# Relative-bias attention followed by hash-routed experts: rows stored in order and gathered through an id table, bias rows written from 128 partitions

## The chip, the cores and the metric

The kernel runs on one core of a Trainium2 chip. The metric is the device time of one execution in microseconds (us). Before the change it is 440.38 us, the median of three runs (440.21 to 440.39).

A core has five engines that run side by side, each with its own queue of instructions, and that wait for each other through semaphores: TensorE (PE, matrix products into PSUM), VectorE (DVE), ScalarE (ACT), GpSimd (POOL) and SyncE (SP, here only for issuing DMAs). DMAs are issued from the queues of SP, ACT and POOL and are carried out by 16 DMA engines. A DMA with a list of row numbers (an indirect DMA, a gather or a scatter) is issued from POOL.

## What is computed

```python
# q, k, v: [8, 8, 576, 64] float32; bias_table: [32, 8]; token_ids: [4608] int64
# w1: [8, 512, 1024], w2: [8, 1024, 512] float32
scores = scale * np.matmul(q, k.transpose(0, 1, 3, 2))
...
scores = scores + bias.transpose(2, 0, 1)[None, :, :, :]   # by |i - j|, constant from 128 on
attn = np.exp(scores - np.max(scores, axis=-1, keepdims=True))
attn = attn / (np.sum(attn, axis=-1, keepdims=True) + 1e-09)
attn_out = np.matmul(attn, v)
x = np.ascontiguousarray(attn_out.transpose(0, 2, 1, 3)).reshape(B * S, H * D)
expert_idx = token_ids * np.int64(2654435761) % np.int64(E)
for e in range(E):
    mask = expert_idx == e
    h = np.maximum(x[mask] @ w1[e], 0.0)
    out[mask] = h @ w2[e]
```

So 4608 tokens of width 512 come out of attention, and each goes through one of eight experts, chosen by a hash of its id. With eight experts and an odd multiplier, the expert's weights can be permuted or the low three bits of the id taken; the kernel takes the low three bits.

## The kernel before

**Attention half.** The work is cut into 32 pairs of heads (`pairs`, batch by batch, four per batch). For pair n the loop body calls `scores(n, g)` five times: TensorE computes a block of scores into PSUM, and ScalarE takes the exponential into `att` (four times, L406) or `atts` (once, L418). VectorE then multiplies the band near the diagonal by the exponential of the bias (`band`, L439 and L445). Beyond the band the bias is constant and cancels. `av_steps(n - 1)` runs the products with v of the pair before (L472), interleaved into the same body, and VectorE normalises into `x_all` (L482, L483). Further per pair: `load(n + 4)` issues seven DMAs for q, k and v on SP; `cast_k` and `cast_q` on VectorE and `cast_v` on ScalarE turn them to float16 two and three pairs ahead; `transpose_q` and `transpose_k` bring them into place through PSUM slots named `aux`, of which there are two. `load_vs` and `cast_vs` (SP and POOL, L218) bring the last 64 rows of v for the next batch.

**Order.** The attention half is emitted under a manual schedule for all five engines: each engine runs its instructions in the order in which the program writes them. An instruction that waits holds up what follows in its own queue, and nothing else. An engine whose instructions wait for nothing runs ahead of the loop body in which they are written.

**The bias.** The table is expanded to 8 rows (one per head), its exponential taken (`ebsb`, L580), and each row written 64 times, with a shift that grows by one element, into the DRAM tensor `t5_f` (L586, two DMAs of 512 KB, from 8 partitions, on ACT's queue). Reading `t5_f` back with another stride gives the diagonal bands `ebd` and `ebs` (L602 and L607, eight DMAs on SP). They stand on SP ahead of `load(2)` and `load(3)`, and `cast_k(2)`, `cast_q(2)` and `cast_q(3)` stand on VectorE ahead of most of pair 0's bands.

**Routing.** `route_load` (pair 4) fetches the low words of the ids, 4 bytes at a time, into `te` with tokens on partitions. `route` (a generator, one step for each `scores` call in pairs 6 to 11) computes the expert of each token and its rank within the expert, and from these the slot `ds2` of each of the 40 groups of 128 tokens. An expert has 640 slots.

**Rows to experts.** `x_all` rows carry two extra float16 columns that hold the token's number. Ten DMAs (`fill_table`, L629, pairs 2 to 11, on SP) fill the table `t5_xperm` in DRAM with zero rows and an impossible number. `dispatch` (L498, 40 indirect DMAs on POOL, two per pair from pair 12) scatters x rows of finished batches to their slots; the last five follow the last pair. In the expert half `x_load` (L724, on SP) reads the 640 slots of an expert as one block, `x_transpose` turns it (L738, L742), TensorE computes both layers (L759, L777), and each block of 128 result rows is scattered to `out` (L785, 40 indirect DMAs on POOL) with the numbers that came along in the row. Weights are loaded and cast by POOL's DMAs (L132, L138); experts 0 and 1 during attention (pairs 20, 22, 25, 28), later ones two experts ahead.

A last part, under `tc.If(over > 0)`, serves tokens beyond 640 of an expert. With these inputs it doesn't run.

Of the kernel before, what the change touches and what calls it, by code (L numbers as in the profile page):

```python
# [31 lines left out]
def kernel(  # L32
# [28 lines left out]
    NROW = NSLOT + N  # L61
# [5 lines left out]
    XW = DM + 2  # L67
# [28 lines left out]
    TOK_np = TOK_np.reshape(P, NGT)  # L96
# [8 lines left out]
    TOK_d = nc.inline_tensor(TOK_np, "t5_tok")  # L105
# [3 lines left out]
    F_d = nc.dram_tensor("t5_f", [H * P + 1, PW], F16, kind="Internal")  # L109
    xperm_d = nc.dram_tensor("t5_xperm", [NROW, XW], F16, kind="Internal")  # L110

# [4 lines left out]
    tok = cst.tile([P, NGT], I32, name="tok")  # L116
# [37 lines left out]
    with tc.tile_pool(name="at", bufs=1) as at, tc.tile_pool(  # L154
# [7 lines left out]
        x_all = at.tile([P, B, NIT, XW], F16, name="x_all")  # L162
# [7 lines left out]
        te = at.tile([P, NGT], I32, name="te")  # L170
# [76 lines left out]
        def route_load():  # L247
            tid32 = moe_token_ids.bitcast(I32)
            for t in range(NIT):
                tk = tok_of[i_first[t] : i_first[t] + P]  # L250
                p0 = 0
                while p0 < P:
                    p1 = p0 + 1
                    while p1 < P and tk[p1] == tk[p1 - 1] + 2:
                        p1 += 1
                    nc.sync.dma_start(
                        out=te[p0:p1, B * t : B * t + B].unsqueeze(2),
                        in_=bass.AP(tid32.tensor, 2 * int(tk[p0]),
                                    [[4, p1 - p0], [2 * S, B], [1, 1]]),
                    )  # L260
                    p0 = p1

        def route():
            nc.gpsimd.tensor_copy(
                out=x_all[:, :, :, DM:XW].bitcast(I32),
                in_=tok[:, :].rearrange("p (t b) -> p b t", b=B).unsqueeze(3),
            )
            nc.vector.tensor_scalar(
                out=te[:, :], in0=te[:, :], scalar1=E - 1, scalar2=None,
                op0=ALU.bitwise_and,  # L270
            )
            yield
            nc.vector.tensor_tensor(
                out=ef[:, :], in0=te[:, :], in1=msk[:, :NGT], op=ALU.add
# [61 lines left out]
            dlt = at.tile([P, NGT], F32, name="dlt")  # L336
            nc.vector.scalar_tensor_tensor(
                out=dlt[:, :], in0=tok[:, :], scalar=float(NSLOT),
                in1=sel[:, :], op0=ALU.add, op1=ALU.subtract,
            )  # L340
            yield
            nc.vector.tensor_tensor(
                out=dlt[:, :], in0=dlt[:, :], in1=ovf[:, :], op=ALU.mult
            )
            yield
            nc.vector.tensor_tensor(
                out=ds2[:, :], in0=dlt[:, :], in1=sel[:, :], op=ALU.add
# [149 lines left out]
        def dispatch(b, t):  # L497
            sc_in = nc.gpsimd.indirect_dma_start(  # L498
                out=xperm_d.ap()[:, :],
                out_offset=bass.IndirectOffsetOnAxis(  # L500
                    ap=ds2[:, B * t + b : B * t + b + 1], axis=0
                ),
                in_=x_all[:, b, t, :],
                in_offset=None,
                bounds_check=NROW - 1,
                oob_is_err=False,
            )
            disjoint(sc_in, "xrows")
# [13 lines left out]
        for hh in range(2):  # L522
            nc.scalar.dma_start(
                out=tbl[:, :, hh : hh + 1],
                in_=bias_table[:, NPAIR * hh : NPAIR * hh + NPAIR].unsqueeze(2),
            )
        ohsb = at.tile([NB, FW], F32, name="ohsb")
        nc.scalar.dma_start(out=ohsb[:, :], in_=OH_d.ap())
        nc.scalar.dma_start(out=ident[:, :], in_=I128_d.ap())

# [42 lines left out]
        for i in range(2):  # L573
            nc.tensor.matmul(
                out=bps[:H, i, :FH],
                lhsT=tbl[:, :, :].rearrange("n m h -> n (m h)"),
                rhs=ohsb[:, FH * i : FH * i + FH],
            )
        ebsb = at.tile([H, 2, FH], F16, name="ebsb")
        nc.scalar.activation(  # L580
            out=ebsb[:, :, :], in_=bps[:H, :2, :FH], func=AF.Exp, bias=0.0,
# [3 lines left out]
        for r in range(2):  # L585
# [3 lines left out]
                    [[P * PW, H], [2 * PW + 1, D], [1, 2 * FY]],  # L589
                ),  # L590
                in_=ebf[:, (1 - r) * FY : (3 - r) * FY]
                .unsqueeze(1).to_broadcast([H, D, 2 * FY]),
            )
        transpose_q(0)
# [4 lines left out]
        for hh in range(2):  # L599
            for o in range(2):  # L600
                f0 = hh * P * PW + o * FY + MAXD // 2 - 1
                nc.sync.dma_start(  # L602
                    out=ebd[:, :, hh, o, :],
                    in_=bass.AP(F_d.ap().tensor, f0,
                                [[PW, P], [2 * P * PW, NPAIR], [1, WB]]),
                )
                nc.sync.dma_start(  # L607
                    out=ebs[D * hh : D * hh + D, :, o, :],
                    in_=bass.AP(F_d.ap().tensor, f0,
                                [[PW, D], [2 * P * PW, NPAIR], [1, UB]]),  # L610
                )
        load(2)
        load(3)
        cast_vs(0)
# [5 lines left out]
        nc.sync.dma_start(out=tok[:, :], in_=TOK_d.ap())  # L620
        zx = at.tile([P, 4, XW], F16, name="zx")
        nc.gpsimd.memset(zx[:, :, :DM], 0.0)
        nc.gpsimd.memset(zx[:, :, DM:XW].bitcast(I32), BIG)

        FILLS = 10

        def fill_table(i):
            rows = NSLOT // FILLS
            nc.sync.dma_start(  # L629
                out=xperm_d.ap()[rows * i : rows * (i + 1), :].rearrange(  # L630
                    "(p r) d -> p (r d)", p=P
                ),
                in_=zx[:, :, :].rearrange("p r d -> p (r d)"),
            )

        NP = len(pairs)
        waiting = []
        routing = route()

        def finish(its):  # L640
            for t in its:
                dispatch(B - 1, t)

        for n in range(NP + 1):
# [8 lines left out]
            if n == 4:  # L653
                route_load()
            if 2 <= n < 2 + FILLS:
                fill_table(n - 2)
# [7 lines left out]
            if n >= 5 and pairs[n - 1][1] == 0:  # L664
                waiting += [(pairs[n - 5][0], t) for t in range(NIT)]
            if n >= 12:
                for _ in range(2):
                    if waiting:
                        dispatch(*waiting.pop(0))
# [8 lines left out]
            for g in range(NIT):  # L678
                scores(n, g)
                if 6 <= n < 12:  # L680
                    next(routing, None)
                if g == 0:
                    if 0 < n < NP - 1:
# [16 lines left out]
                elif g == 3:  # L700
                    if n == 0:
                        transpose_q(1)
                        transpose_k(1)
# [8 lines left out]
        assert not waiting  # L712
        guard.__exit__(None, None, None)

    with tc.tile_pool(name="mo", bufs=1) as mo, tc.tile_pool(
# [6 lines left out]
        def x_load(e):  # L722
            xpn = mo.tile([P, NSC, XW], F16, name="xpn", bufs=3)
            nc.sync.dma_start(  # L724
                out=xpn[:, :, :],
                in_=xperm_d.ap()[ts(e, CAP), :].rearrange(
                    "(sc p) d -> p sc d", p=P
                ),
            )
# [15 lines left out]
        with tc.manual_schedule(engines={mybir.EngineType.SP}):  # L745
            xn = {0: x_load(0)}
# [182 lines left out]
```

## Time and profile before

| what | value |
|---|---|
| median of three runs | 440.38 us |
| the profiled execution, its own time | 437.86 us |
| its span, first to last instruction | 436.0 us |
| TensorE busy | 334.5 us (77%) |
| VectorE busy | 225.9 us (52%) |
| ScalarE busy | 219.7 us (50%) |
| POOL busy | 106.8 us (24%) |
| attention half | up to about 263 us |
| expert half, from the first transpose of a block (L738) | from 275.53 us |

The rows that follow are the page's second part: the span in 40 slices of 10.9 us, one digit for each. A digit is the busy share of the slice in tenths, 9 being 90% or more. `DMA` is the mean busy share of the 16 DMA engines, and `GB/s` what they moved.

```profile
PE   4120788789865585898888780799999999999991
ACT  1110699889954495898889680133150422404220
POOL 2020010000056125041322204014335053350421
DMA  7438789899999468779799102548999999998211
```

The rows show four parts: a start of some four slices in which hardly anything is busy but the DMA engines; an attention part with dips in slices 12 to 16 and 23; a bridge of about two slices (25 and 26); and an expert part in which TensorE is always busy. A busy share is no limit by itself: in the attention part VectorE and ScalarE are both near full where the pace is steady, and the pace of a pair is read from ScalarE's exponentials.

### The profile page before, as it was taken

The numbers are of one execution on the slowest core, as the hardware profiler recorded it, in microseconds if no ns is written. First come the engines' busy times: TensorE is split into PE (matmuls) and PEld (weight loads), VectorE is DVE, ScalarE is ACT, GpSimd is POOL, SyncE is SP. The second block draws the span as 40 slices with busy tenths as digits, with TensorE's granted clock in tenths as the row PEclk, the third lists the DMA queues.
The fourth block names the chain that finished last, engine by engine and source line by source line (L and its number), as shares of the span: only waits on it lengthen the run. The fifth ranks groups of instructions, "written<-read, shape, count | busy, mean of one in ns | idle before, by whom it ended". The sixth has DMA issues, their size and how long they took to land. (4 is left out here: it accounts for less than half of the span.)

```text
span 436.0 us, 8653 instructions
## 1 busy us (share of the span) xinstructions
PE 334.5 (77%) x3398; PEld 238.0 (55%) x3398; DVE 225.9 (52%) x608; ACT 219.7 (50%) x258; POOL 106.8 (24%) x135
## 2 busy tenths in 40 slices
PE   4120788789865585898888780799999999999991
PEld 1010677667744474776667570566575665656550
DVE  4001699999953594898989561121413223142221
ACT  1110699889954495898889680133150422404220
POOL 2020010000056125041322204014335053350421
PEclk9999999999996697999999897699999999999997
DMA  7438789899999468779799102548999999998211
GB/s 171 61 44 205 186 212 161 215 251 248 247 226 252 106 163 183 179 158 215 185 208 172 43 2 65 172 68 196 162 241 244 164 256 156 251 213 164 108 50 71
DMA packets 130803, 72.75 MB, mean 167 GB/s; under 512 B 88992, under 2 KB 121888, under 8 KB 130753
## 3 DMA queue, kind: packets, MB, share of 16 engines
q1 hardware_dynamic: 111568, 39.97, 39.4%
q0 software_dynamic: 17664, 30.96, 33.3%
q10 hardware_dynamic: 1520, 1.18, 2.1%
q8 instruction: 28, 0.46, 0.4%
q14 instruction: 23, 0.18, 0.1%
HBM read 68.38 MB, written 22.06 MB: 207 GB/s over the span
## 5 line engine op out<-in xcount | busy, mean ns | idle before, releaser
L406 ACT ACTIVATE att<-ps 128x1152 f16<-128x1152 f32 x128 | 140.7, 1128 | 44.4 <-remote 15.5
L398 PE MATMUL ps<-qt,kz 128*128 128x384 f16 x256 | 78.1, 344 | 34.7 <-ACT att L406 30.7
L765 ACT ACTIVATE h<-hps 128x640 f16<-128x640 f32 x64 | 45.1, 704 | 113.2 <-PE hps L759 112.5
L472 PE MATMUL px<-vt,att 128*128 128x98 f16 x1280 | 84.6, 211 | 2.8 <-issue 1.4
L472 PEld LDWEIGHTS <-att 128*128 128x128 f16 x1280 | 72.4, 101 | 9.0 <-issue 2.8
L759 PE MATMUL hps<-xpt,w1t 128*128 128x320 f16 x512 | 72.8, 303 | 0.0
L777 PE MATMUL ops<-w2t,h 128*128 128x512 f16 x320 | 72.7, 379 | 0.0
L439 DVE TENSOR_TENSOR att<-att,ebd 128x512 f16<-128x512 f16 (+1 forms) x192 | 68.4, 385 | 0.7 <-ACT att L406 0.5
L402 PE MATMUL ps<-qt,kz 128*128 128x192 f16 x256 | 65.7, 257 | 0.0
L759 PEld LDWEIGHTS <-w1t 128*128 128x128 f16 x512 | 50.7, 99 | 21.6 <-issue 0.2
L498 POOL DMA_INDIRECT t_xperm<-x_all,ds x40 | 40.0, 1001 | 82.1 <-DVE x_all L483 40.4
L742 DVE COPY xpt<-xps 128x640 f16<-128x640 f16 x32 | 15.0, 489 | 74.6 <-PE xps L738 73.6
L785 POOL DMA_INDIRECT out_dram<-ok,xpn x40 | 39.2, 980 | 57.4 <-DVE ok L784 50.9
L784 DVE COPY ok<-ops 128x512 f32<-128x512 f32 x40 | 27.7, 692 | 47.0 <-PE ops L777 47.0
L777 PEld LDWEIGHTS <-h 128*128 128x128 f16 x320 | 30.7, 98 | 33.5
L402 PEld LDWEIGHTS <-kz 128*128 128x128 f16 x256 | 25.9, 101 | 40.4 <-issue 39.9
L218 POOL CAST vs<-vsf 64x256 f16<-64x256 f32 x16 | 7.7, 484 | 128.2 <-DMA vsf<-in_v_dram 100.8
L358 PE MATMUL pq<-ident,qh 96*128 96x96 f16 x192 | 14.5, 215 | 29.0 <-DVE qt L366 20.3
L472 PE MATMUL px<-vs,atts 128*128 128x132 f16 x160 | 36.1, 225 | 0.5 <-ACT atts L418 0.3
L240 ACT ACTIVATE vt<-vf 128x512 f16<-128x512 f32 x32 | 19.8, 623 | 31.1 <-DMA vf<-in_v_dram 31.1
L234 DVE CAST kh<-kf 128x640 f16<-128x640 f32 x32 | 15.6, 487 | 34.7 <-DMA kf<-in_k_dram 34.6
L398 PEld LDWEIGHTS <-kz 128*128 128x128 f16 x256 | 26.1, 102 | 13.2 <-issue 2.7
(56 smaller groups left out, 272.9 us busy)
## 6 DMA issues: line engine op xcount, KB each, us to landing
qf<-in_q_dram SPq DMA_DIRECT2D x64, 144.0 KB
kf<-in_k_dram SPq DMA_DIRECT2D x64, 128.0 KB
vf<-in_v_dram SPq DMA_DIRECT2D x64, 128.0 KB
w1t<-in_moe_w_dram POOLq DMA_DIRECT2D x8, 1024.0 KB
w2t<-in_moe_w_dram POOLq DMA_DIRECT2D x8, 1024.0 KB
t_xperm<-zx SPq DMA_DIRECT2D x10, 514.0 KB
xpn<-t_xperm SPq DMA_DIRECT2D x8, 642.5 KB
kf<-in_k_dram SPq DMA_DIRECT2D x32, 32.0 KB
```

The source lines that it names most:

```text
L240: nc.scalar.activation(out=vt[n % 4][:, :].rearrange("p (h y) -> p h y", h=2)[:, :, : NDUO * VN].rearrange("p h (t x) -> p h t x", t=NDUO) ...
L398: nc.tensor.matmul(out=ps[:, hh, :QW], lhsT=kt, rhs=qt[:, :QW], start=True, stop=True,)
L402: nc.tensor.matmul(out=ps[:, 2, RW * hh : RW * hh + RW], lhsT=kt, rhs=qt[:, QW:], start=True, stop=True,)
L406: nc.scalar.activation(out=att[:, g, :, :], in_=ps[:, :, :QW], func=AF.Exp, bias=0.0, scale=scale,)
L439: nc.vector.tensor_tensor(out=a, in0=a, in1=ebd[:, m, :, :, a0 + w0 : a1 + w0], op=ALU.mult,)
L472: nc.tensor.matmul(out=px[:, ii, o : o + w], lhsT=lhsT, rhs=rhs, start=(y == 0), stop=(y == len(todo) - 1), skip_group_check=True,)
L498: sc_in = nc.gpsimd.indirect_dma_start(out=xperm_d.ap()[:, :], out_offset=bass.IndirectOffsetOnAxis(ap=ds2[:, B * t + b : B * t + b + 1], ...
L759: nc.tensor.matmul(out=hps[:, nr, :NR], lhsT=w1h[:, kt, ts(ft, P)], rhs=xt[e][:, kt, ts(nr, NR)], start=(kt == 0), stop=(kt == NPT - 1),)
L765: nc.scalar.activation(out=h1[:, ft, :].rearrange("p (r n) -> p r n", r=NRC), in_=hps[:, :, :NR], func=AF.Relu, bias=0.0, scale=1.0,)
L777: nc.tensor.matmul(out=ops[:, :], lhsT=h1[:, ft, ts(kc, P)], rhs=w2h[:, ft, :], start=(ft == 0), stop=(ft == NFT - 1),)
L784: nc.vector.tensor_copy(out=ok[:, :], in_=ops[:, :])
L785: so = nc.gpsimd.indirect_dma_start(out=out[:, :], out_offset=bass.IndirectOffsetOnAxis(ap=xn[e][:, kc, DM:XW].bitcast(I32), axis=0), in_= ...
```

## The change

- **Bias.** The table is repeated to 128 columns (`tblr`: eight heads, 16 copies), so the exponential comes out on 128 partitions. Each partition writes 4 shifted rows to `t5_f`. The bytes are the same. The reading back is split: `load_bias(0, 1)` for the first head pair of each batch, then `load(2)`, then `load_bias(1, NPAIR)`, then `load(3)`, eight DMAs for each `load_bias`. `cast_vs(0)` and, in pair 0, `transpose_q(1)` and `transpose_k(1)` move forward.
- **Ids.** One DMA on ACT's queue loads all ids as 8 rows (`raw`). VectorE masks them, converts them to float16, and TensorE transposes them (`tps`). `route` runs from pair 2 to 7, and its last three steps become one.
- **Rows.** `x_all` loses its two extra columns. Finished batches are stored in token order into `t5_x` by SP (`store`, two DMAs a batch, three for the last). A small table `t5_id` of 5120 slots with two numbers each is filled with an impossible number in one DMA. `name_slot` scatters the pair (row number, token number) of each of the 40 groups into it: 40 indirect DMAs on POOL, three per pair from pair 8. In pair 24 SP loads the table back as `xid`.
- **Expert half.** `x_load` becomes five indirect gathers on POOL per expert, from `t5_x` into one of three tiles `xg`, which are zeroed at the start. The result scatter takes its numbers from `xid`. The manual schedule for SP around the first two loads goes.

```diff
-    F_d = nc.dram_tensor("t5_f", [H * P + 1, PW], F16, kind="Internal")
-    xperm_d = nc.dram_tensor("t5_xperm", [NROW, XW], F16, kind="Internal")
+    NRP = P // H
+    RPW = P // (2 * NRP)
+    PP = RPW * (2 * PW + 1)
+    HPF = NRP * PP
+    F_d = nc.dram_tensor("t5_f", [P + 1, PP], F16, kind="Internal")
+    x_d = nc.dram_tensor("t5_x", [N, DM], F16, kind="Internal")
+    id_d = nc.dram_tensor("t5_id", [NSLOT, 2], I32, kind="Internal")
...
-        def route_load():
...
+        def route():
+            for h0, w, u0 in ((0, UA, 0), (QW, UB, UA)):
+                nc.vector.tensor_scalar(
+                    out=te[:, h0 : h0 + 2 * w].rearrange(
+                        "b (o u) -> b o u", o=2
+                    ),
+                    in0=raw[:, :, 0].rearrange("b (u o) -> b o u", o=2)[
+                        :, :, u0 : u0 + w
+                    ],
+                    scalar1=E - 1, scalar2=None, op0=ALU.bitwise_and,
+                )
+            yield
+            nc.gpsimd.memset(tef[:, :].bitcast(I32), 0)
+            nc.vector.tensor_copy(out=tef[:B, :], in_=te[:, :])
+            yield
+            tps = aux([P, NIT, P], F16, "tps")
             for t in range(NIT):
...
+                nc.tensor.transpose(
+                    out=tps[:, t, :], in_=tef[:, i_first[t] : i_first[t] + P],
+                    identity=ident[:, :],
+                )
...
-        def dispatch(b, t):
-            sc_in = nc.gpsimd.indirect_dma_start(
-                out=xperm_d.ap()[:, :],
+        def name_slot(g):
+            i = nc.gpsimd.indirect_dma_start(
+                out=id_d.ap()[:, :],
                 out_offset=bass.IndirectOffsetOnAxis(
-                    ap=ds2[:, B * t + b : B * t + b + 1], axis=0
+                    ap=ds2[:, g : g + 1], axis=0
                 ),
-                in_=x_all[:, b, t, :],
+                in_=pay[:, g, :],
                 in_offset=None,
-                bounds_check=NROW - 1,
+                bounds_check=NSLOT - 1,
                 oob_is_err=False,
             )
...
+        def store(b, t0, t1):
+            xv = x_d.ap()[S * b : S * b + S, :]
+            t2 = min(t1, NDUO)
+            nc.sync.dma_start(
+                out=xv[P * t0 : P * t2, :].rearrange("(t p) d -> p t d", p=P),
+                in_=x_all[:, b, t0:t2, :],
+            )
+            if t1 > NDUO:
+                nc.sync.dma_start(
+                    out=xv[NB4:, :], in_=x_all[P - S + NB4 :, b, NDUO, :]
+                )
...
-                    [[P * PW, H], [2 * PW + 1, D], [1, 2 * FY]],
+                    [[PP, P], [2 * PW + 1, RPW], [1, 2 * FY]],
                 ),
                 in_=ebf[:, (1 - r) * FY : (3 - r) * FY]
-                .unsqueeze(1).to_broadcast([H, D, 2 * FY]),
+                .unsqueeze(1).to_broadcast([P, RPW, 2 * FY]),
...
+        cast_vs(0)
+        load_bias(0, 1)
         load(2)
+        load_bias(1, NPAIR)
         load(3)
-        cast_vs(0)
...
+        nobody = at.tile([P, NSLOT // P, 2], I32, name="nobody")
+        nc.gpsimd.memset(nobody[:, :, :], BIG)
+        nc.sync.dma_start(
+            out=id_d.ap().rearrange("(p g) c -> p (g c)", p=P),
+            in_=nobody[:, :, :].rearrange("p g c -> p (g c)"),
+        )
+        for i in range(3):
+            nc.gpsimd.memset(xg[i][:, :, :].bitcast(I32), 0)
...
         def finish(its):
-            for t in its:
-                dispatch(B - 1, t)
+            store(B - 1, its[0], its[-1] + 1)
...
-            if n == 4:
-                route_load()
-            if 2 <= n < 2 + FILLS:
-                fill_table(n - 2)
...
             if n >= 5 and pairs[n - 1][1] == 0:
-                waiting += [(pairs[n - 5][0], t) for t in range(NIT)]
-            if n >= 12:
-                for _ in range(2):
-                    if waiting:
-                        dispatch(*waiting.pop(0))
+                store(pairs[n - 5][0], 0, NIT)
+            if n >= 8:
+                for g in unnamed[:3]:
+                    name_slot(g)
+                del unnamed[:3]
+            if n == 24:
+                nc.sync.dma_start(
+                    out=xid[:, :, :],
+                    in_=id_d.ap().rearrange("(g p) c -> p g c", p=P),
+                )
...
         def x_load(e):
-            xpn = mo.tile([P, NSC, XW], F16, name="xpn", bufs=3)
-            nc.sync.dma_start(
-                out=xpn[:, :, :],
-                in_=xperm_d.ap()[ts(e, CAP), :].rearrange(
-                    "(sc p) d -> p sc d", p=P
-                ),
-            )
+            xpn = xg[e % 3]
+            for sc in range(NSC):
+                nc.gpsimd.indirect_dma_start(
+                    out=xpn[:, sc, :],
+                    out_offset=None,
+                    in_=x_d.ap()[:, :],
+                    in_offset=bass.IndirectOffsetOnAxis(
+                        ap=xid[:, NSC * e + sc, 0:1], axis=0
+                    ),
+                    bounds_check=N - 1,
+                    oob_is_err=False,
+                )
             return xpn
```

## The prediction

> **What bounds the kernel now.** I read the slices and the chain of waits first, then stretches of equal pace, then the order of time in the two places where the pace breaks.
>
> ```profile
> 262.56 0.32 POOL t_xperm L498
> ...
> 267.67 2.42 DMA t_xperm<-x_all,ds
> ...
> 270.52 4.36 DMA xpn<-t_xperm
> 274.88 0.66 issue
> 275.53 0.70 PE xps L738 x5
> ```
>
> The chain reaches back only to 260 us. From 275.53 on it is TensorE without gaps (the expert half, 152 us). Between the halves lies a bridge: five scatters, a landing, a load, 13 us. What precedes must be read by pace. Each head pair issues four `att` exponentials (L406), one `atts` and one `vt`: 4 x 1.13 + 0.65 + 0.62 = 5.8 us of ScalarE.
>
> ```profile
> core 0: us, ACT busy (x), PEclk, DMA share, GB/s
> 55.80:79.10 23.30, 17.61 (x16) 1.00 0.90 186
> 79.10:105.10 26.00, 17.61 (x16) 1.00 1.01 241
> 105.10:122.50 17.40, 13.21 (x12) 1.00 0.97 243
> 122.50:149.30 26.80, 8.93 (x8) 0.78 0.98 217
> 149.30:162.00 12.70, 8.80 (x8) 0.92 0.49 119
> 162.00:180.10 18.10, 8.92 (x8) 0.81 0.88 191
> 180.10:234.40 54.30, 39.44 (x36) 1.00 0.90 187
> 234.40:255.50 21.10, 13.21 (x12) 0.92 0.30 63
> ```
>
> These are L406 alone by stretch; four are one pair. First row: 4 pairs in 23.3 us, 5.8 each, so there ScalarE is the limit, with the DMA engines 0.90 busy. The last five rows hold 72 = 18 pairs, worth 104.4 us, in 133.0: 28.6 us too many. In that stretch lie 35 of the 40 row scatters (L498).
>
> ```profile
> 137.77 0.62 ACT L240 ACTIVATE vt<-vf 128x512 f16<-128x512 f32 x1
> 145.99 2.15 ACT L406 ACTIVATE att<-ps 128x1152 f16<-128x1152 f32 x2 [7.59 <-remote]
> ```
>
> ScalarE stands for 7.59 us while POOL issues eight scatters back to back (134.40 to 144.41, one per 1.28 us); TensorE's last matmul for that tile began at 138.13. The runs differ: 14 scatters in runs of six and eight lie where 15.2 us are lost, six (and a weight load) where 6.5 are lost, so 1.08 each; ten in runs of one to three cost 0.2 each; five in one run 3.7 us, 0.74 each. The mean is 28.6/35 = 0.8. What stands still is TensorE's word to the others.
>
> The Trainium skill ("SBUF — State Buffer", Who interferes with whom) says that TensorE and ScalarE wait on nobody, and that DMAs never contend with compute engines. The 7.59 us disagree. By that rule small scatters would be free and the sum 401, which is a rival below.
>
> ```profile
> 8.71 11.88 ACTq L586 DMA_DIRECT2D t_f<-ebsb  x2
> 20.68 1.15 ACT L240 ACTIVATE vt<-vf 128x512 f16<-128x512 f32 x2 [12.01 <-DMA vf<-in_v_dram]
> ...
> 42.95 0.63 ACT L240 ACTIVATE vt<-vf 128x512 f16<-128x512 f32 x1 [19.07 <-DMA vf<-in_v_dram]
> ...
> 51.12 1.13 ACT L406 ACTIVATE att<-ps 128x1152 f16<-128x1152 f32 x1 [1.51 <-PE ps L402]
> ```
>
> ```profile
> 31.79 0.38 SPq L602 DMA_DIRECT2D ebd<-t_f  x1
> ...
> 36.64 0.60 SPq L185 DMA_DIRECT2D qf<-in_q_dram  x1
> ```
>
> The third place is the start. The bias rows (2 x 512 KB from 8 partitions) are issued at 8.71, and SP gets past its wait for them at 31.79: 23.1 us, 45 GB/s. ACT's queue is held, and on SP everything behind the wait is late: load(2), for which VectorE waits until 41.72, and load(3), until 44.80. Steady work begins with the exponential at 51.12.
>
> **The change, part by part.** The sum is made against the profiled execution, 437.86 us with 436.0 of span. The median of the runs is 440.38; I add the difference, 2.5.
>
> *Bias rows from 128 partitions.* Same bytes. At the best slice's 252 GB/s they take 4.2 us, at the expert load's pace (642.5 KB in 4.36 us, 151 GB/s) 7.0; the upper end is the 23.1 of now, if the partitions were not the limit. I take 5.8, landing at X = 14.5 us, since other full-width transfers here run at such rates. Behind X, SP issues eight bias loads for pair 0 (31.79 to 36.64 now: 4.85), load(2) (4.06), eight more bias loads (4.85), and load(3), whose second q part is issued 1.56 later and lands 2.54 after that (42.26 to 44.80 now). `cast_q(3)` stands ahead of band(0,1) on VectorE, so pair 0 goes on at X + 17.9, where it now goes on at 31.79 + 13.0. From there to the exponential of 51.12 it is 6.3 us, of which 1.35 (the copies of pair 1, now emitted earlier) are already done: X + 22.9 = 37.4, gain 13.7. Four small loads delay load(4) by 0 to 1: I take **-13.2** (bounds -15 and, without any faster write, +4).
>
> The skill ("DMA: Bandwidth & Descriptors", Rules for kernel authors) says that an outermost size of 8 keeps a DMA on at most 8 of 16 engines. By engine count alone the write would halve to 11.5 us, and the sum would be 437; the trace has no such write to compare.
>
> *Small work at the start:* the `tblr` copy, the token load on ACT's queue (0.5 us), three memsets of `xg` on POOL (128x1280 int32, about 1.4 us each by the 0.45 of vt's 128x424 at L539). 0: the tables wait for `ohsb` until 5.13, ACT stands idle from 4.02 to 7.88, and POOL is idle after 24; uncovered they would cost 0.5 and 4 us.
>
> *Routing moves from pairs 6 to 9 to pairs 2 to 4.* It now costs 26.0 - 23.2 = 2.8 us in the second stretch. New are two integer masks and a conversion on 8 partitions, five transposes and a copy out of a slot shared with q and k; gone are three small VectorE operations. **+1.0**, between 0 and 2.
>
> *The zero fill (10 x 514 KB) and the eight token loads go.* 0: the pace is 5.8 with fills, in the first and third stretch. Bounds 0 to -2.8, what the second stretch lost. What the fill did set is when scatters may begin (123.0).
>
> *Stores in order* add 17 SP issues of about 0.5 us, and SP waits at each for the last x_all of its batch. Behind it stand load(n+4): SP spends 4.2 us a pair on loads, has 1.6 to spare without fills, and a load issued in pair n is used in pair n+1 or later. 0; a lost cover would cost up to 4 us a batch. The id table's load (8-byte pieces) is at pair 24: like the token loads, which SP issued for 5.9 us without the pace breaking. 0, at most 3.
>
> *The 40 row scatters become 40 id scatters*, same kind of instruction, rows of 8 bytes for 1028. POOL waits for nothing between them but the casts of vs (L218), so three per pair in the program become runs of 9, 12, 12 and 7, from pair 5 on. Bounds: free, which leaves the 0.2 each of the short runs' stretch for its weight loads, -26.5; or POOL's full 1.28 us less two free ones in each run, 40 x 1.28 - 4 x 1.28 = 46, +17.4. The longer runs speak for the dear end, the small rows for the cheap one, and the expert half too: there L785 scatters, three of them 1.3 us apart, leave TensorE without a gap. I take the mean price of all 35: 40 x 0.8 = 32, **+3.6**.
>
> *The bridge.* The last x_all is written at 262.94. Two stores of 0.5, landing like the scatter in 2.42: 266.4. Five gathers of 1.28: last issued at 271.6, landing after 2.42 (like a scatter) to 4.36 (like the load), plus 0.66: 274.7 to 276.6. TensorE may begin on the first chunk. **-0.8**, between -3 and +1.1.
>
> *In the expert half* 40 gathers, 1.28 us each, join POOL's queue. Behind them stand w1 loads and scatters. Five take 6.4 us, and POOL now stands 6.5 to 6.7 us per expert ahead of L132; the first fifteen end near 285, before 288.65. 0; if they held TensorE's word as in the run of five, 3.7 us per expert.
>
> Sum: 437.86 - 13.2 + 1.0 + 3.6 - 0.8 = 428.5; with 2.5, **431**. Its own range, id scatters at 0.55 to 1.0 each, is 421 to 439.
>
> **Rivals.**
> - *Id scatters are free* (data, not issue, made the stall): 437.86 - 13.2 + 1.0 - 26.5 - 0.8 + 2.5 = 401. For: the scatters of the expert half. Against: five scatters stopped ScalarE with the DMA engines 0.30 busy.
> - *Slower: long runs cost POOL's full time.* Place: pairs 5 to 18; price 1.08 to 1.15 each. Everything else gains 13.0, so it decides from (28.6 + 13.0)/40 = 1.04 per scatter. At 1.08 to 1.15: 437.86 - 13.0 + 14.6 (or 17.4) + 2.5 = 442 to 445, say 443. For: all runs of six and more.
> - *Gathers stop the expert half:* +29, 460.
> - *The bias write isn't faster:* start +4 instead of -13.2, 448. Against: 45 GB/s is far from any other large transfer.
>
> **How the numbers follow.** Forecast 43 in 100, free 24, slower by long runs 26, gathers 4, bias write 3. About 0.2% is what a measurement of this kernel can tell from no change. Faster 0.63 (nearly all of the first two), same 0.05, slower 0.32. The predicted time is the likeliest case's, 431. The range, 402 to 448, leaves out half of the free case and the gathers' case.
>
> **What would show it.** Bias wait on SP ending near 14.5, and exponentials at full pace from about 38. ScalarE's idle pieces beside the id scatters: some 32 us in all; none would mean the free case, over 40 the slower one. Between the last x_all and the first transposes, 12 us. L759 and L777 without gaps. The prediction is wrong first of all where id scatters cost other than 0.8 each.

## The result and the profile after

The changed kernel takes **474.64 us** (median of four runs, 473.38 to 482.27) beside 440.38 for the kernel before in the same comparison (440.21 to 441.65): a ratio of 1.0775, 95% interval 1.0732 to 1.0818. The profiled execution is the longest of the four, 482.27 us with a span of 480.3, so its terms together are some 8 us larger than the median's.

Its second part, the span in 40 slices (12.0 us each):

```profile
PE   4338783844853867888849915497999898999990
ACT  2136683933943866999947801112240404314210
POOL 2400034072063052010200047454457372441430
DMA  7477776463554549997792033157669788997211
```

Read POOL against ACT, counting slices from 1. The runs of id scatters are POOL's 3 and 4 (slices 6 and 7), 7 and 2 (9, 10), 6 and 3 (12, 13), 5 and 2 (15, 16). ACT shows 3 in slice 7, 3 and 3 in 9 and 10, 4 and 3 in 12 and 13, 6 and 6 in 15 and 16, and 8 or 9 between. PE is no longer a row of nines in the expert part.

The start, in order of time on ACT and SP (start, duration, engine, line, operation, and in brackets the idle time before it and what ended it):

```profile
9.32 1.55 ACTq L611 DMA_DIRECT2D t_f<-ebsb  x2
...
16.04 0.35 SPq L624 DMA_DIRECT2D ebd<-t_f  x1
...
30.43 1.13 ACT L407 ACTIVATE att<-ps 128x1152 f16<-128x1152 f32 x1 [0.66 <-PE ps L403]
37.46 1.13 ACT L407 ACTIVATE att<-ps 128x1152 f16<-128x1152 f32 x1 [5.90 <-PE ps L403]
```

SP is past its wait for the bias rows at 16.04 (31.79 before), and the exponential that stood at 51.12 stands at 37.46.

One run of twelve id scatters in the same view, POOL first, then TensorE and ScalarE:

```profile
134.96 1.02 POOL L499 DMA_INDIRECT t_id<-pay,ds  x1 [0.28 <-POOL vs L230]
136.28 0.97 POOL L499 DMA_INDIRECT t_id<-pay,ds  x1 [0.30 <-issue]
...
149.01 0.97 POOL L499 DMA_INDIRECT t_id<-pay,ds  x1 [0.30 <-issue]
```

```profile
137.23 0.25 PE L403 MATMUL ps<-qt,kz 128*128 128x192 f16 x1
...
139.38 0.24 PE L403 MATMUL ps<-qt,kz 128*128 128x192 f16 x1
143.15 0.66 PE L359 MATMUL pq<-ident,qh 96*128 96x96 f16 x6 [3.52 <-remote]
...
137.80 1.13 ACT L407 ACTIVATE att<-ps 128x1152 f16<-128x1152 f32 x1 [1.61 <-PE ps L403]
138.82 0.62 ACT L252 ACTIVATE vt<-vf 128x512 f16<-128x512 f32 x1
146.59 1.13 ACT L407 ACTIVATE att<-ps 128x1152 f16<-128x1152 f32 x1 [7.15 <-remote]
152.35 1.13 ACT L407 ACTIVATE att<-ps 128x1152 f16<-128x1152 f32 x1 [4.63 <-remote]
```

The exponentials read TensorE's blocks in order. The block read at 146.59 was finished by TensorE at 137.48, the one read at 152.35 at 139.63, as the trace has it. No instruction or DMA that ends just then accounts for the end of these waits, hence "remote". Between 134.96 and 152.35 three exponentials (L407) begin, where 17.4 us have room for twelve. Such a standstill is a stop in what follows.

What ScalarE waits for is TensorE's semaphore, and the trace also keeps the times at which a semaphore was raised. Seven of TensorE's matmuls that raise it end in this stretch, at 136.35, 136.99, 137.48, 139.63, 143.81, 144.57 and 148.41. It is raised seven times, at 137.78, 142.28, 146.57, 152.33, 152.41, 152.51 and 152.55. The exponentials of 137.80, 146.59 and 152.35 begin 0.02 us after the first, the third and the fourth of these. So TensorE's signals come late, by up to 12.7 us, one every 4 to 6 us while the run lasts and the last four together, 2.3 us after the last scatter has left POOL (149.98). The ends of matmuls are modelled, so the trace can't tell a late signal from a late last result.

The same in the expert part, where gathers (L750) go out in a row of twenty, from 280.8 to 306.7:

```profile
299.29 0.70 ACT L793 ACTIVATE h<-hps 128x640 f16<-128x640 f32 x1 [3.42 <-remote]
307.76 0.70 ACT L793 ACTIVATE h<-hps 128x640 f16<-128x640 f32 x1 [7.77 <-remote]
...
308.52 1.76 PE L787 MATMUL hps<-xpt,w1t 128*128 128x320 f16 x6 [6.20 <-ACT h L793]
```

The sums, from the table of waits (engine, what waited, for what; us in total, times, longest):

```profile
ACT att L407 <- remote: 25.4, 5, 7.1
...
PE hps L787 <- ACT h L793: 18.1, 10, 6.2
DVE qt L367 <- remote: 15.3, 2, 7.9
...
DVE rcp L483 <- remote: 14.3, 2, 9.0
...
ACT h L793 <- remote: 12.7, 4, 7.8
```

In the expert part TensorE now waits for ScalarE, which waits for TensorE's signal; before, L759 and L777 had no gaps.

The longer expert part has two pieces. From its first to its last product TensorE stands idle for 18.9 us (before: 0.0), and it is busy for 158.5 us instead of 149.1, with a mean granted clock of 0.92 instead of 0.99. The granted clock is 0.50 from 300.1 to 313.8; TensorE's first three waits there end at 295.9, 300.0 and 308.5. The signals of the blocks that TensorE ended at 297.17 and 302.32 are raised at 307.74 and 309.21, and ScalarE begins on them at 307.76 and 309.24.

From the profile before to the one after, by stages (starts of the pairs' first exponentials, first and last products of the expert part):

| stage | before | after | difference |
|---|---|---|---|
| to pair 5 | 73.30 | 64.45 | -8.9 |
| pair 5 to pair 31 | 182.2 | 205.8 | +23.6 |
| pair 31 to the first product of a first layer | 21.8 | 20.1 | -1.7 |
| from there to the last product of a second layer | 149.2 | 177.4 | +28.2 |
| to the end of the span | 9.5 | 12.6 | +3.1 |

### The profile page after: what moved, and what is told of

The parts are those of the page before. It is cut to its first block, busy times and chain, and to the rows that moved or that the text cites. A ratio compares the mean times of both kernels' runs of the same rounds, so it can differ in the third digit from the quotient of the medians.

```text
span 480.3 us, 8733 instructions
## 1 busy us (share of the span) xinstructions
PE 349.2 (73%) x3403; PEld 244.7 (51%) x3403; DVE 226.8 (47%) x609; ACT 220.0 (46%) x258; POOL 150.5 (31%) x177
## 4 chain that ended last, share of the span: by engine, by line
PE 46%; ACT 11%; issue 8%; SPq 8%; DMA 8%; another core or an unknown queue 8%; DVE 6%; DVEq 2%; ACTq 0%; POOLq 0%; POOL 0%
PE hps L787 17%; PE ops L805 14%; ACT att L407 8%; PE px L473 5%; PE ps L399 4%; DMA qf<-in_q_dram 2%; ACT vt L252 2%; PE xps L768 2%; DVEq L772 2%; PE ps L403 2%; DVE att L440 2%; SPq L203 2%; DMA vsf<-in_v_dram 1%; DMA vf<-in_v_dram 1%
## 5 line engine op out<-in xcount | busy, mean ns | idle before, releaser
L407 ACT ACTIVATE att<-ps 128x1152 f16<-128x1152 f32 x128 | 141.2, 1128 | 79.2 <-PE ps L403 31.6
L399 PE MATMUL ps<-qt,kz 128*128 128x384 f16 x256 | 79.5, 348 | 34.1 <-ACT att L407 26.0
L787 PE MATMUL hps<-xpt,w1t 128*128 128x320 f16 x512 | 82.2, 322 | 18.9 <-ACT h L793 18.1
L473 PE MATMUL px<-vt,att 128*128 128x98 f16 x1280 | 86.1, 214 | 7.4 <-DVE qt L367 4.2
L473 PEld LDWEIGHTS <-att 128*128 128x128 f16 x1280 | 74.1, 102 | 13.4 <-DVE qt L367 4.4
L787 PEld LDWEIGHTS <-w1t 128*128 128x128 f16 x512 | 53.5, 105 | 47.0 <-issue 21.4
L230 POOL CAST vs<-vsf 64x256 f16<-64x256 f32 x16 | 9.6, 599 | 166.3 <-DMA vsf<-in_v_dram 84.5
L750 POOL DMA_INDIRECT xg<-t_x,xid x40 | 40.5, 1012 | 55.1 <-DMA t_x<-x_all 41.5
L813 POOL DMA_INDIRECT out_dram<-ok,xid x40 | 39.8, 994 | 42.9 <-DVE ok L812 35.5
L499 POOL DMA_INDIRECT t_id<-pay,ds x40 | 39.2, 980 | 12.1 <-issue 11.0
L484 DVE TENSOR_TENSOR x_all<-px,rcp 128x384 f16<-128x384 f32 x64 | 31.4, 491 | 2.2
```

The costliest lines, as they stand in the source:

```text
L399: nc.tensor.matmul(out=ps[:, hh, :QW], lhsT=kt, rhs=qt[:, :QW], start=True, stop=True,)
L407: nc.scalar.activation(out=att[:, g, :, :], in_=ps[:, :, :QW], func=AF.Exp, bias=0.0, scale=scale,)
L473: nc.tensor.matmul(out=px[:, ii, o : o + w], lhsT=lhsT, rhs=rhs, start=(y == 0), stop=(y == len(todo) - 1), skip_group_check=True,)
L484: nc.vector.tensor_tensor(out=x_all[:, b, its[0] : its[0] + ni, :DM].rearrange("p t (h m d) -> p t h m d", h=2, m=NPAIR)[:, :, :, m, :], i ...
L499: i = nc.gpsimd.indirect_dma_start(out=id_d.ap()[:, :], out_offset=bass.IndirectOffsetOnAxis(ap=ds2[:, g : g + 1], axis=0), in_=pay[:, g, ...
L750: nc.gpsimd.indirect_dma_start(out=xpn[:, sc, :], out_offset=None, in_=x_d.ap()[:, :], in_offset=bass.IndirectOffsetOnAxis(ap=xid[:, NSC * ...
```

## The experiments

The runs come in five groups; a group ran on one chip, together with the kernel before. **The groups met three chips.** Chip A (third group) gave the kernel before 438.09 us. Chip B (first, second and fourth) gave it 422.4 to 423.4, chip C (fifth) 422.6. The chip of the first comparison is not recorded; by its 440 it is like A. In the recorded expectations, "a chip with stops" is one like that, and "without stops" one like B.

**Group 1, chip B: the changed kernel again, then one part at a time.**

> The changed kernel itself, once more, for a second profile of it. Both theories: 474 us. It shows whether the stops beside the runs of id scatters (9.0, 15.0, 14.9 and 8.1 us lost), the 8.3 us lost in pair 28 and the 26 us lost in the expert half are there again: expected are the same places and sizes within 1 us each, since nothing differs.

Measured 418.8 (one execution), against 423.44 before. The four stops, and those of the expert part, are gone, with the same instructions. The run of twelve here:

```profile
94.25 0.97 POOL L499 DMA_INDIRECT t_id<-pay,ds  x1 [0.30 <-issue]
95.52 1.18 POOL L499 DMA_INDIRECT t_id<-pay,ds  x1 [0.31 <-issue]
97.01 0.97 POOL L499 DMA_INDIRECT t_id<-pay,ds  x1 [0.30 <-issue]
...
95.91 2.14 ACT L407 ACTIVATE att<-ps 128x1152 f16<-128x1152 f32 x2
97.93 0.66 ACT L419 ACTIVATE atts<-ps 128x576 f16<-128x576 f32 x1
98.84 1.13 ACT L407 ACTIVATE att<-ps 128x1152 f16<-128x1152 f32 x1 [0.25 <-ACT atts L419]
100.17 1.13 ACT L407 ACTIVATE att<-ps 128x1152 f16<-128x1152 f32 x1 [0.20 <-PE ps L403]
```

POOL issues 1.27 to 1.5 us apart as on the other chip, and ScalarE goes on at 5.81 us a pair. No wait in this profile is put down to "remote", and before the kernel's last instructions no signal of TensorE's is raised more than 0.1 us after a matmul's end.

```diff
-            if n >= 8:
-                for g in unnamed[:3]:
-                    name_slot(g)
-                del unnamed[:3]
+        def paced(n, it, i):
+            b, m = pairs[n]
+            nc.gpsimd.tensor_copy(
+                out=pc[:1, i : i + 1], in_=x_all[:1, b, it, D * m : D * m + 1])
+            name_slot(unnamed.pop(0))
...
                     band(n, 1)
+                    if n >= 5 and unnamed:
+                        paced(n - 1, 0, 2 * n)
```

The same stands after `band(n, 2)`, with 3 for 0, and the id table is loaded in pair 25.

> The changed kernel with all 40 id scatters, but each behind a one-element GpSimd copy of a value that VectorE writes twice per head pair, so that two scatters of one pair are some 2.9 us apart instead of 1.28. Theory (while indirect DMAs follow each other on GpSimd without a pause, TensorE's signals reach the others late; a pause lets them through): the 47 us lost beside the runs shrink to 40 x 0.2 = 8 or less, so 474 - 39 to 474 - 47, 427 to 435. Rival (each indirect DMA costs about 1.18 us wherever it stands): no change, 474; the pacing copies may even add a few us. Rival (DMA traffic in that stage made the stops): no change.

420.33 (0.989, 0.981 to 0.998): nothing to gain on this chip.

```diff
+                if e + 2 < E and ft in (1, 2, 4, 5, 7):
+                    nc.gpsimd.tensor_copy(out=pd[...], in_=h1[:1, ft, :1])
+                    x_gather(e + 2, GAT.index(ft))
```

> The changed kernel with the 30 gathers of experts 2 to 7 held back one by one: each stands behind a one-element GpSimd copy of a hidden block that ScalarE has just written, five in the eight blocks of an expert; the ten of experts 0 and 1 stay one run. GpSimd's order in the expert half is the program's. Theory: the 26 us lost in the expert half shrink to what the run of ten leaves, 10 x 1.28 less the 6 us that lie in the bridge, 5 to 8 us; total 474 - 18 to 474 - 21, 453 to 456. Rival (each gather costs its share wherever it stands, 26/40 = 0.65 us): no change, 474.

422.22 (0.996, 0.991 to 1.000): nothing to gain here either.

```diff
-            if n == 24:
+            if n == 28:
                 nc.sync.dma_start(out=xid[:, :, :], ...
```

> The changed kernel with the load of the id table (5120 pieces of 8 bytes) issued by SyncE in pair 28, behind the last loads of q, k and v, instead of pair 24. Theory: it held up the q and v loads behind it, which is the 8.3 us that pair 28 lost; so 474 - 8 = 466. Rival (w2's weight load of pair 28 is what held them up): the loss stays, 474.

416.56 (0.982, 0.973 to 0.991), the quickest of the group, and some 3 us below the changed kernel itself in groups 2 and 4 on the same chip (419.57 and 420.16). The expectations suppose a chip with stops, so the runs with spacing decide nothing about it here.

**Group 2, chip B: is it the chip?**

> The kernel before itself, for a profile of it on the chip of this group. On the chip of the first comparison it took 440 and lost 28.6 us in pairs 13 to 30 beside its row scatters; on the chip of the first group of experiments it took 423 and no profile of it was made. If the stops belong to the chip: either 440 with about 28 us of ScalarE's idle time beside the scatters, or about 423 with nearly none there. If they belong to the program: 440 with them, on any chip.

423.67. Pairs 13 to 18, in which 34.9 us at full pace had become 57.6 in the first profile of this kernel, take 5.81 each. What is lost lies in pairs 7, 23, 27 and 29 (3.7 to 4.2 us each), the later three mostly to q loads, for which VectorE waits 9.6 us.

> The changed kernel itself against the kernel before. If the stops belong to the chip: 474 against 440 where the chip has them (ratio 1.08), about 419 against 423 where it doesn't (ratio 0.99). If the 419 of the first group came from something else of that hour: any other pairing.

419.57 (0.994, 0.989 to 0.9998).

> The changed kernel with the 40 id scatters spaced as in the run with paced names, the 30 gathers of experts 2 to 7 spaced as in the run with paced gathers, and the id table loaded in pair 28. On a chip with stops, theory (a pause between indirect DMAs lets TensorE's signals through): 474 - 39 - 18 = 417 or a little less. On a chip without stops: about 419, since there is nothing to let through. Rival (on a chip with stops the price of an indirect DMA is the same wherever it stands): 474.

416.24 (0.992, 0.988 to 0.995), within 3 us of what was expected here.

The bias part alone on the kernel before (`tblr`, the new layout of `t5_f`, `load_bias`, and pair 0's moves, as in the change's diff):

> The kernel before with only the bias part of the change: the table repeated to 128 columns, rows written from 128 partitions, the reading back split, and the moves of pair 0 that go with it. From the changed kernel's profile (the second pair began at 30.4 instead of 48.5 and its pace was reached 14 us earlier): the time of before less 13 on a chip with stops, where nothing behind is bound by transfers. Rival (what is won at the start is given back, because loads of q, k, v and weights bind later pairs): less than 5 us won.

413.69 (0.987, 0.978 to 0.997): by the medians 8.7 us gained, between the theory's 13 and the rival's 5. By the two profiles pair 5 begins 12.5 us earlier and pair 31 12.6, so little is given back there; the profiled execution of the kernel before is 1.3 us above its median, that of this kernel 1.6 below.

**Group 3, chip A: the chip with stops.** Here the kernel before took 438.09 (434.49 to 440.77).

The changed kernel without its bias part:

> The changed kernel with the bias rows written from 8 partitions as before, in the old order of loads and of pair 0: all of the change but its first part. If the parts add up, on the chip of the first two groups: 422 + (419.6 - 413.7) = 428, so slower than before by 1 to 2 per cent. On a chip with stops: 474 + 13 = 487. Rival (the rows part is worth nothing or a gain by itself): 422 or less on the chip without stops.

**484.9** (1.107, 1.097 to 1.117), for an expected 487. The stops are back; its waits:

```profile
ACT att L403 <- remote: 23.0, 5, 7.7
DVE qt L363 <- remote: 21.3, 3, 9.6
...
DVE rcp L479 <- remote: 13.1, 3, 5.7
...
ACT h L779 <- remote: 12.9, 3, 4.9
```

Names and gathers spaced, the id table in pair 28, and the weights earlier:

```diff
-            if n == 20:
+            if n == 6:
                 load_w1(0)
```

The other three weight loads move from pairs 22, 25 and 28 to 11, 16 and 21.

> The changed kernel with names and gathers spaced and the id table loaded in pair 28, as before in this study, and with the four weight loads of experts 0 and 1 begun in pairs 6, 11, 16 and 21 instead of 20, 22, 25 and 28. On the chip of the first two groups the DMA engines are 0.79 busy from 60 to 160 us and 1.06 from 163 to 200, where pairs 24 and 28 stand 8.3 and 3.2 us for q. Theory (what binds the late pairs there is the total of the transfers, and earlier weights spread it): the 13 us lost in pairs 24 to 29 go, 416 - 13 = 403, give or take 3. Rival (the pairs then stand for q wherever the weights go): 416. On a chip with stops: the same or less than 417, since the spacing holds there too, if the theory on spacing is right.

**419.45** (0.962, 0.952 to 0.971). All of its waits for "remote" are one:

```profile
DVE rcp L483 <- remote: 2.4, 1, 2.4
```

Its scatters and exponentials, in order of time:

```profile
113.44 1.00 POOL L499 DMA_INDIRECT t_id<-pay,ds  x1 [0.15 <-issue]
...
114.77 0.97 POOL L499 DMA_INDIRECT t_id<-pay,ds  x1 [0.16 <-issue]
117.44 0.31 POOL L527 COPY pc<-x_all 1x1 f16<-1x1 f16 x1 [1.70 <-DVE x_all L484]
118.16 1.34 POOL L499 DMA_INDIRECT t_id<-pay,ds  x1 [0.41 <-issue]
...
121.12 0.97 POOL L499 DMA_INDIRECT t_id<-pay,ds  x1 [0.54 <-issue]
...
116.45 1.13 ACT L407 ACTIVATE att<-ps 128x1152 f16<-128x1152 f32 x1 [1.69 <-PE ps L403]
...
120.92 1.13 ACT L407 ACTIVATE att<-ps 128x1152 f16<-128x1152 f32 x1 [0.25 <-ACT atts L419]
122.63 1.13 ACT L407 ACTIVATE att<-ps 128x1152 f16<-128x1152 f32 x1 [0.58 <-PE ps L403]
```

POOL was late here and caught up with four scatters 1.3 to 1.6 us apart, from 110.56 to 114.77, and the pair that began at 113.63 lost 1.5 us. The next pair, with scatters 3 us apart, lost 0.4. The four have the same copies between them, so the copy is not what helps; this speaks for the distance. The stages side by side, in us, from the starts of exponentials and the products of the expert part:

| stage | after, first comparison | rows alone, A | all spaced, A | after, B |
|---|---|---|---|---|
| pairs 6 to 18 (75.5 us at full pace) | 122.4 | 121.6 | 82.8 | 78.7 |
| expert part, first to last product | 177.4 | 172.4 | 150.5 | 149.1 |

On one and the same chip, of the 46 us lost in pairs 6 to 18 all but 7 go, and in the expert part 22 go. The two kernels differ in the bias part, the id table's place and the weights as well; the next experiment leaves the last two as they were. The total stays 2 us above the 417 expected at most: pairs 9, 19 and 24 lose 2.7 to 4.0 us, the last two mostly to q loads.

The kernel before, with the bias part, and its row scatters spaced in the same way:

> The kernel before with the bias part of the change, and its 40 row scatters each behind a one-element GpSimd copy of a value that VectorE writes twice per pair, so two per pair and never three in a row. On a chip with stops, theory (spacing lets TensorE's signals through): 440 - 13 - 20 = 407. Rival (price per scatter): 427. On the chip of the first two groups, without stops: nothing to gain by spacing, 414 like the bias part alone, 2 either way.

**407.35** (0.930, 0.919 to 0.941), where 407 was expected. No wait for "remote" is left in its profile, and no signal of TensorE's stands more than 2.4 us behind a matmul's end that it can belong to. Pairs 13 to 30 lose 6.7 us, where the first profile of the kernel before lost 28.6.

**Groups 4 and 5, chips B and C: again.** The parts were to be told apart on a chip with stops, which neither group met.

> The changed kernel itself, as the base of this group. On a chip with stops 474 against 440; on one without 419 against 422.

420.16 (0.999, 0.994 to 1.004).

> The changed kernel with only its 40 id scatters spaced, the same kernel as in the first group. On a chip with stops: 474 less the 47 us beside the runs, plus 40 x 0.2 to 0.3 that single scatters still cost there: 435 to 439 if nothing else moves. Rival (the runs are not what the 47 us belong to): 474. On a chip without stops 420 again.

> The changed kernel with only the 30 gathers of experts 2 to 7 spaced, the same kernel as in the first group. On a chip with stops: of the 26 us lost in the expert half the run of ten gathers leaves 5 to 8, so 474 - 18 to 474 - 21, 453 to 456. Rival (a gather costs its share wherever it stands): 474. On a chip without stops 422 again.

419.91 (0.997, 0.992 to 1.001) and 422.33 (1.001, 0.996 to 1.006): as in group 1.

> The kernel before with the bias part and its row scatters spaced, the same kernel as in the third group. On a chip with stops 407 again, against 440. On a chip without: 414, as the bias part alone gave there, 2 either way, so the fastest or as fast as any on both.

**407.27** (0.970, 0.964 to 0.977), 7 us less than expected on this chip. It beats both kernels on B and the kernel before on A, where the changed kernel as it is was not run. Why spacing the row scatters gains 6 us over the bias part alone (406.56 to 409.44 against 410.77 to 415.69) on a chip without stops was not followed up; by the two profiles 2.9 us of it lie in pairs 13 to 30. So not all of the 20 us that spacing was expected to give on A need come from the stops.

> The changed kernel with only its id scatters spaced, a third time, for a chip with stops: 435 to 439 there by the theory, 474 by the rival; 420 on a chip without.

> The changed kernel with only the gathers of experts 2 to 7 spaced, a third time, for a chip with stops: 453 to 456 there by the theory, 474 by the rival; 422 on a chip without.

> The changed kernel with only the id table's load moved from pair 24 to pair 28. On a chip with stops pair 28 lost 8.3 us in the changed kernel's profile: if the id table's load held up the q and v loads behind it, 474 - 8 = 466; if w2's weight load did, 474. On a chip without stops 417 again.

On chip C: 420.74 (0.995, 0.991 to 0.999), 420.39 (0.998, 0.994 to 1.001) and **415.86** (0.985, 0.979 to 0.992). The kernel with the later id table takes 415.06 to 417.34, the two others 416.78 to 423.46, some 4.5 us more. But those have spaced names or gathers, and the changed kernel itself was not run on C; on B the id table's place is worth some 3 us beside it. On a chip with stops it was not tried alone. The load in the first profile after, on SP's queue:

```profile
226.56 0.37 SPq L692 DMA_DIRECT2D xid<-t_id  x1
227.03 3.81 SPq L197 DMA_DIRECT2D qf<-in_q_dram  x1
```

The 5120 pieces of 8 bytes cost SP itself 0.37 us, and the next q load's issue 3.81, where the median of this profile's q loads after 60 us is 0.50. Others of them take up to 3.44 with no id table ahead of them; but the load behind the id table takes 2.6 to 8.8 us in every profile that has one there. Pair 28, which uses what is loaded there, took 14.06 us for 5.81. How much of these 8.3 us is the id table's isn't settled: with the table in pair 24 pair 28 loses 3.5 to 8.3 us in the profiles of all chips, with the table in pair 25 10.8 to 11.7, and with the table in pair 28, behind the loads, still 3.2 to 3.9. Where the weights were moved as well (group 3), it loses nothing, so w2's load, issued in pair 28, may have the rest.

## Why the prediction was wrong

It said 431 and the comparison 474.6. By its own steps, in the two profiles:

- **Bias rows, -13.2: right.** X was 16.04 for 14.5, the steady exponential 37.46 for 37.4, so -13.7. The write took 6.7 us from its issue at 9.32, the 23.1 of before divided by more than three. The Trainium skill ("DMA: Bandwidth & Descriptors", Rules for kernel authors) has an outermost size of 8 confine a DMA to at most 8 of the 16 engines; an estimate by that count alone is half the time, and here it was less than a third.
- **Routing, +1.0: right.** Pairs 2 to 4 took 4.1 us over their pace, the old routing 2.8: +1.3. **Bridge, -0.8: right.** From the last x_all to the first full transpose 12.2 us for 12.6.
- **The id table's load, "0, at most 3": probably too small.** Pair 28 loses 8.3 us in the profile, and part of that is the table's (on B, loading it later gained some 3 us). It was counted by what SP spends on it, not by how long the load behind it takes.
- **The id scatters, 40 x 0.8 = 32: the first wrong size.** The runs came as foreseen, 9, 12, 12 and 7. Pairs 6 to 18 lost 47 us beside them, 1.18 each: 9.0 in the run of nine, 15.0 and 14.9 in the two of twelve, 8.1 in the seven, so nearly POOL's full 1.28 in the longest. I had taken the mean over runs of one to eight; the rows of six and eight alone gave 1.08. The term was +18.4, not +3.6. The loss of 47 lies just above the upper bound of 46.
- **The gathers in the expert half, "0": the step that failed.** It was argued from POOL's spare time and from scatters that cost nothing there. But most of those stand 1.73 us apart, and no order by hand keeps the new ones so: twenty gathers went out in one run, and later ones between the scatters. Beside them TensorE's signals come late here too, and the expert part is 28.2 us longer, 18.9 of them TensorE standing and the rest its products at a lower granted clock, which the prediction had nowhere. The rival that priced this at +29 had 4 in 100; that its number fits is partly luck, since it counted stops alone, 3.7 us for each of eight experts.

Together: 437.86 - 13.7 + 1.3 + 18.4 + 8.3 - 0.4 + 28.2 = 480.0, with the 3.1 at the end of the span, for which the prediction had no term, 483.1, against 482.27. The 8.3 is all of pair 28's loss, whatever caused it. The two dear rivals were kept apart as 26 and 4 in 100, as though one excluded the other. By the late signals they are one cause in two places, and both came true: if long runs of indirect DMAs cost POOL's time, they do so wherever they stand. Together they gave 443 + 29 = 472.

**What is shown.** On a chip with stops, scatters on POOL 1.3 us apart cost nearly their whole duration in the long runs, TensorE's signals are recorded late beside them, and spacing them takes both away. Two spaced kernels of group 3 show it. One has the id table and the weights moved as well. The other has only the bias part beside the spacing, and the bias part alone can't be the cure, since the changed kernel has it and stops. For the gathers there is only the first of these two. The stores of finished batches are no rival: they are issued as the runs begin (96.7, 134.9, 173.1 us), but also at 205.5 and 236.0, where no scatters stand beside them and the pairs keep their 5.81 us.

**What stays open:** why the signals are late; how the gain divides between names and gathers, other than by the stages' sums; and whether the stops belong to the chip or to the occasion, since chip A was met once.

On chip B the change is worth next to nothing (0.994 and 0.999): the bias part alone takes 413.69, the whole change 419.57, so the rows part gives back some 6 us, about 3 of which a later load of the id table gains back.

## What to carry to other kernels

Where a profile shows such stops, give each indirect DMA on GpSimd a pause of its own: tie it to a value that another engine produces at a steady pace, some 3 us apart, and look at what a queue that waits for nothing makes of "three per pair". Where a stall's price depends on the length of a run, price the longest runs, and apply it in every place with such runs; rivals that share a cause are not alternatives. A gain or a loss of this kind is worth a second chip before it is believed.

## What the runs showed of the hardware

- The changed kernel, with its id scatters in runs of up to twelve, lost 47 us in pairs 6 to 18 in the first comparison, and 2 to 5 there in three profiles on chip B. The mean granted clock of the kernel before, 0.952 in the first comparison and 0.936 on B, doesn't tell them apart. That of the changed kernel does: 0.876 to 0.898 in the first comparison, 0.923 to 0.954 on B.
- In the stops it is TensorE's semaphore that is raised late, by up to 12.7 us. With the row scatters spaced, on chip A, no raising is later than 2.4 us; on chip B, with the long runs, none is later than 0.1.
- On the chip with stops the size of the rows made no difference that shows: 1028 bytes (before) and 8 bytes (after) gave 1.08 and 1.18 per scatter in long runs, and gathers stop the expert part too. The Trainium skill ("SBUF — State Buffer", Who interferes with whom) has TensorE and ScalarE wait on nobody, as a rule on SBUF ports. The 7.15 us of above are a wait for a late signal, which a rule on ports doesn't cover, so the prediction's "disagree" says too much. The profiles of chips B and C show no such wait.
